# Rebuilding the front of a DFT and MLP kernel: x loads first, one casting queue for the weights, a turn by chunks of lines, and a low-rank step in column tiles

## The chip, the cores and the metric

The kernel runs on one core of one Trainium2 chip. The metric is the device time of one execution in microseconds (us). Most executions of one kernel agree within a few tenths of a per cent; the median is quoted with its range. "Faster" or "slower" means by more than 2%. The "granted clock" is the share of TensorE's full speed that the chip allowed, as the trace records it; the "span" runs from the first to the last instruction of the profiled execution.

## The reference

For eight sequences of 3136 rows and 256 columns the reference takes the real part of a two-dimensional DFT, adds a low-rank mix along the sequence, and then a two-layer MLP with a residual:

```python
def reference(x, U, V, w_ch1, w_ch2):         # x (8, 3136, 256); U (3136, 32); V (32, 3136)
    X = np.fft.fft(np.fft.fft(x, axis=1), axis=2).real
    u = X + ((X.transpose(0, 2, 1) @ U) @ V).transpose(0, 2, 1)
    return u + np.maximum(u @ w_ch1, 0) @ w_ch2       # w_ch1 (256, 1024), w_ch2 (1024, 256)
```

## The kernel before

The 3136-point DFT is split as 49 times 64. Four names recur in the profile:

- `xs -> ps -> z`: stage 1. The first pair of sequences is loaded sequence by sequence, each in four chunks, by loads that cast f32 to bf16. The Trainium skill ("DMA: Bandwidth & Descriptors", section "SWDGE vs HWDGE vs iDMA") says that only DMAs issued from GpSimd can cast. In this trace all casting loads are in one queue, q0; the transfers that SP issues are in q1.
- `z -> zturn -> g`: the turn. z is written to HBM and read back with the other axis on the partitions.
- `teps -> te`: the low-rank step on TensorE, copied ("spread") into the lower half of g. Its weights are made from U: `us` for a single sequence, and `UZ`, the same values sent through HBM (`uturn`), for a pair.
- `g, T -> ps -> q`, then `hps -> hT -> ops -> om -> out`: stage 3 and the MLP.

The front, which is everything before the first MLP matmul (hps), is a hand-made order. Here are the parts that matter, with cuts marked:

```python
    nc.sync.dma_start(out=U_f, in_=moe_U...)            # plain f32, SP's queue
    nc.sync.dma_start(out=uv[64:96], in_=moe_V)
    part[0][1] = load_single(0, 1)                      # x of sequence 0: casting loads from GpSimd
    part[0][2] = load_single(0, 2)
    ...                                                 # chunks 3 and 0; GpSimd: copies of V into T, iotas, mask
    s1b0[2](); s1b0[3]()                                # stage 1; every second step writes z to zturn
    nc.sync.dma_start(out=w1_f[:], in_=moe_w_ch1...)    # W1 behind the first z writes on SP's queue
    ...
    s1b0[6](); s1b0[7]()
    ...
    nc.vector.tensor_tensor(w1s[:, 0], w1_f[:, 0], w1_f[:, 1], op=AL.add)
    nc.vector.tensor_tensor(w1s[:, 1], w1_f[:, 0], w1_f[:, 1], op=AL.subtract)
    turn(first, 0, [(0, 8), (8, 16), (16, NK1)], [nc.sync, nc.scalar])   # read g, after all z writes
    keep_warm(8)
    ...                                                 # W1 fold on TensorE; W1p out
    bp_sin = residual_tables()
    nc.gpsimd.tensor_copy(w2_f[0:64, 0, 0, 0:3], first.g[0][0:64, 7:NK1:8, 0])   # W2 waits for g
    nc.sync.dma_start(out=w2_f, in_=moe_w_ch2...)
    te_single(first, 0, spread_first)                   # low-rank step, then stage 3
    ...
    for c in (1, 2, 3, 0):
        part[1][c] = load_single(1, c)                  # x of sequence 1, behind the copy that waits for g
```

`keep_warm` issues matmuls whose results nobody uses, to keep TensorE busy; `residual_tables` makes the sine table `Bp` of the residual's matmuls (`ops<-Bp,q`). The low-rank step multiplies cosine and sine parts together and masks what is not wanted:

```python
    for j in range(lo, hi):                             # one pair of sequences: 32 matmuls of 256 columns
        nc.tensor.matmul(st.ps[:, 0, :], UZ[:, j], pr.z[:, j], start=(j == 0), stop=(j == 31))
    ...
    nc.vector.tensor_tensor(te[64:128, :], ps[hb, 0, :], mask[hb, :], op=AL.mult)
```

Of the kernel before, what the change touches and what calls it, by code (L numbers as in the profile page):

```python
# [8 lines left out]
BF16 = mybir.dt.bfloat16  # L9
# [13 lines left out]
def kernel(  # L23
# [19 lines left out]
    ud = nc.dram_tensor("uturn", (NK1, 2, 32, 64), BF16, kind="Internal").ap()  # L43
# [14 lines left out]
    Fs = cpool.tile([PR, 9, 32, 2], FP16)  # L58
# [9 lines left out]
    mask = cpool.tile([P, D], FP32)  # L68
# [117 lines left out]
    def s1_single(pr, b, tiles, evacs, engines):  # L186
# [5 lines left out]
        zdb = zd[pr.p % 2, b]  # L192

        def step(n, s):
# [3 lines left out]
            for i in range(2):  # L198
                o = ps[64 * i:64 * i + 64]
                if s == 0 and i == 0:  # L200
                    todo.append([(o[:, 1], xs[:, 1], 0), (o[:, 0], xs[:, 0], 1), (o[:, 0], x32[b][:], 2)])
                else:
                    todo.append([(o, xs[:, l + 2 * i:l + 2 * i + 2], 0)])
            prods = []
            for parts in todo:
                pp = []
                for o, y, t in parts:
                    fe, fo, fn = (Fs[:, 3 * t + i].rearrange("p k c -> p (k c)") for i in range(3))
                    pp += [(o[..., 0:129], fe, y[..., 0:129]), (o[..., 1:128], fe, y[..., 255:128:-1]),
                           (o[..., 129:256], fo, y[..., 1:128]), (o[..., 129:256], fn, y[..., 255:128:-1])]  # L210
                prods.append(pp)
# [6 lines left out]
            if n % 2:  # L218
                q = s // 2
                for i in range(2):  # L220
                    dst = bass.AP(zd.tensor, zdb.offset + (8 * q + 2 * i) * D, [[32 * D, 64], [4 * D, 2], [1, 2 * D]])
                    engines(n)[i].dma_start(out=dst, in_=z[64 * i:64 * i + 64, 4 * q:4 * q + 4].rearrange(
                        "p (i h) d -> p i (h d)", h=2))
# [4 lines left out]
    def turn(pr, b, parts, engines=(nc.sync,)):  # L228
        g = gpool.tile([P, NK1, D], BF16, tag=f"g{b}", name="g")
        src = zd[pr.p % 2, b].rearrange("k cn d -> cn k d")  # L230
        for i, (k0, k1) in enumerate(parts):
            engines[i % len(engines)].dma_start(out=g[0:64, k0:k1], in_=src[:, k0:k1, :])
        pr.g[b] = g

    def te_out(pr, b, ps, hb, spread):
        te = ypool.tile([P, D], BF16, tag="te", name="te")
        nc.vector.tensor_tensor(te[64:128, :], ps[hb, 0, :], mask[hb, :], op=AL.mult)  # L237
        spread(pr.g[b], te)

    def te_steps(pr, spread):  # L240

        st = Obj()

        def step(lo, hi):
            if lo == 0:
                st.ps = psd.tile([P, 2, D], FP32, tag="ps", name="teps")
            for j in range(lo, hi):
                nc.tensor.matmul(st.ps[:, 0, :], UZ[:, j], pr.z[:, j], start=(j == 0), stop=(j == 31))  # L248
            if hi == 32:
                for b in range(2):  # L250
                    te_out(pr, b, st.ps, slice(64 * b, 64 * b + 64), spread)

        for lo, hi in [(0, 11), (11, 22), (22, 32)]:
            yield lambda lo=lo, hi=hi: step(lo, hi)

    def te_single(pr, b, spread):

        ps = psd.tile([P, 2, D], FP32, tag="ps", name="teps")
        for k in range(NK1):
            nc.tensor.matmul(ps[0:64, 0, :], us[:, k], pr.g[b][0:64, k, :], start=(k == 0), stop=(k == NK1 - 1))  # L260
        te_out(pr, b, ps, slice(0, 64), spread)
# [144 lines left out]
    uv = tmp([P, S], "uv")  # L406
    U_f = uv[0:64, 0:N1 * R]
    nc.sync.dma_start(out=U_f, in_=moe_U.rearrange("(k2 k1) r -> k2 (k1 r)", k1=N1))
    nc.sync.dma_start(out=uv[64:96], in_=moe_V)
    first = Pair(0)  # L410
    part = [[None] * 4, [None] * 4]
    part[0][1] = load_single(0, 1)
    part[0][2] = load_single(0, 2)
    an2 = tmp([PR, 2, 3, 32, 2], "an2")
    nc.gpsimd.memset(an2[:], 192.0)
    part[0][3] = load_single(0, 3)
    nc.gpsimd.memset(x32[0][:].bitcast(FP32), 0.0)
    part[0][0] = load_single(0, 0)

    Vk = uv.rearrange("p (k2 k1) -> p k1 k2", k1=N1)  # L420
    for lo, hi in [(0, 9), (9, 17), (17, NK1)]:
        nc.gpsimd.tensor_copy(T[64:96, lo:hi, 0:64], Vk[64:96, lo:hi, :])
    kio = UZ[0:64].rearrange("p a b -> p (a b)").bitcast(I32)[:, 0:64 * NK1].rearrange("p (k j) -> p k j", j=64)

    nc.gpsimd.iota(kio, pattern=[[1, NK1], [N1, 64]], base=0, channel_multiplier=0)
    nc.gpsimd.iota(kio[32:33, 0:NK1:2], pattern=[[0, 13], [1, 64]], base=0, channel_multiplier=0)
    nc.gpsimd.iota(kio[32:33, 1:NK1:2], pattern=[[0, 12], [-1, 64]], base=63, channel_multiplier=0)
    nc.gpsimd.memset(mask[:], 0.0)
    for b in range(2):
        nc.gpsimd.memset(mask[64 * b:64 * b + 32, 0:129], 1.0)  # L430
        nc.gpsimd.memset(mask[64 * b + 32:64 * b + 64, 129:256], 1.0)

# [33 lines left out]
    ans = tmp([PR, 3, 32, 2], "ans")  # L466
    for tab, c, off in [(0, 0, 192.25), (0, 1, 192.5), (1, 0, 1), (1, 1, 2), (2, 0, 3), (2, 1, 4)]:
        ts(ans[:, tab, :, c], jf[0:PR, 0:32], pv[:, 0:1], off if off > 100 else pv[:, off:off + 1])
# [5 lines left out]
    ub = tmp([64, N1, R], "ub", BF16)  # L474
    nc.scalar.copy(ub[:].rearrange("p k r -> p (k r)"), U_f)
# [9 lines left out]
    ts(ta[:, :, 0:32], tb[:], 32.25, None, AL.add)  # L485
    ts(ta[:, :, 32:64], tb[:], 32.0, None, AL.add)
    ts(alt[:, 1:2], ph[:], 0.5, 32.25)
    ts(alt[:, 2:3], ph[:], -0.5, 32.75)
    nc.vector.tensor_copy(ta[:, 0:NK1:2, 32], alt[0:64, 1:2].to_broadcast([64, 13]))
    nc.vector.tensor_copy(ta[:, 1:NK1:2, 32], alt[0:64, 2:3].to_broadcast([64, 12]))  # L490
    mask_bits(ta[:], 18)
    ups = psh.tile([P, 2, 512], FP32, tag="h", name="ups")
    for i in range(2):
        nc.tensor.matmul(ups[0:64, i, 0:384], jm[:], ub[:, NK1 + 12 * i:37 + 12 * i].rearrange("p k r -> p (k r)"),
                         start=True, stop=True)
    keep_warm(4)
    rv = tmp([64, 2, 12, 2, R], "rv", BF16)
    ups_v = ups[0:64, :, 0:384].rearrange("p i (k r) -> p i k r", k=12)
    nc.scalar.copy(rv[:, :, :, 0, :], ups_v)
    ua = tmp([64, NK1, 64], "ua", FP16)  # L500
    nc.scalar.copy(T[64:96, 1:NK1, 64:128], Vk[64:96, 48:24:-1, :])



# [4 lines left out]
    ts(jq[:, 0, 65:P], jf[:, 2:P:2], pl[:], 128.5)  # L509
    ts(jq[:, 1, 0:64], jf[:, 1:P:2], pl[:], 128.25)  # L510
    ts(jq[:, 1, 64:P], jf[:, 1:P:2], pl[:], 128.5)
    mask_bits(jq[:], 16)

    w1_f = tmp([P, 2, H], "w1_f")
    A, V = copy_act, copy_dve
    s1b0 = list(s1_single(first, 0, part[0], [A, V, A, V, A, V, A, A],
                          lambda n: (nc.sync, nc.scalar if n == 7 else nc.sync)))
    s1b0[0]()
    sin_of(ua[:], ta[:], 18)
    s1b0[1]()  # L520
    keep_warm(4)
    ts(rv[:, :, :, 1, :], ups_v, -1.0, None)


    ts(m[:], h, -1.0, 1.0)
    ts(pv[:, 5:6], u[:], m[:], None)
    ts(pv[:, 6:7], u[:], 24.0 / 49, m[:], AL.subtract, AL.mult)
    for i, off in enumerate([0.25, 0.0, 0.5]):
        ts(pv[:, 7 + i:8 + i], m[:], off, 192.0)
    s1b0[2]()  # L530
    s1b0[3]()
    nc.sync.dma_start(out=w1_f[:], in_=moe_w_ch1.rearrange("(h p) j -> p h j", p=P))
    keep_warm(4)
    for i in range(2):
        for t in range(3):
            ts(an2[:, i, t, :, i], jf[0:PR, 0:32], pv[:, 5 + i:6 + i], pv[:, 7 + t:8 + t])
    mask_bits(an2[:], 16)
    Q = tmp([P, 2, P], "Q", FP32R)
    sin_of(Q[:], jq[:], 16)
    sin_of(Fs[:, 3:9], an2[:].rearrange("p a t k c -> p (a t) k c"), 16)  # L540


    pn = tmp([64, 2], "pn")
    ts(pn[:, 1:2], pf[0:64], 32.0, 32.0, AL.is_ge, AL.mult)
    ts(pn[:, 0:1], pf[0:64], pn[:, 1:2], 1.0 / S, AL.subtract, AL.mult)
    ts(pn[:, 1:2], pn[:, 1:2], -0.25 / 32, 32.25)
    nc.vector.memset(pn[32:33, 0:1], 0.5)
    nc.vector.memset(pn[32:33, 1:2], 32.25)
    ta2 = kio.bitcast(FP32)
    s1b0[4]()  # L550
    s1b0[5]()
    ts(ta2, kio, pn[:, 0:1], pn[:, 1:2])
    mask_bits(ta2, 18)

    for k0, k1 in [(0, 16), (16, 25)]:
# [9 lines left out]
        if k0:  # L565
            copy_dve(us[:, k0:k1], ps[0:64, 0:k1 - k0])
        else:
            ups0 = ps
    s1b0[6]()
    s1b0[7]()  # L570
    copy_act(us[:, 0:16], ups0[0:64])
    nc.vector.tensor_copy(T[96:128, :, 0:64], T[64:96, :, 0:64])
    ts(T[96:128, 1:NK1, 64:128], T[64:96, 1:NK1, 64:128], -1.0, None)
    w1s = tmp([P, 2, H], "w1s", FP32R)
    nc.vector.tensor_tensor(w1s[:, 0], w1_f[:, 0], w1_f[:, 1], op=AL.add)
    nc.vector.tensor_tensor(w1s[:, 1], w1_f[:, 0], w1_f[:, 1], op=AL.subtract)
    turn(first, 0, [(0, 8), (8, 16), (16, NK1)], [nc.sync, nc.scalar])
    sin_of(T[0:64, :, 0:64], ta2, 18)
    nc.vector.tensor_copy(T[0:64, :, 64:128], T[0:64, :, 63::-1])
    keep_warm(8)  # L580

    for c in range(2):
        cs = slice(c * 512, (c + 1) * 512)
        ps = psh.tile([P, 2, 512], FP32, tag="h", name="w1ps")
        for blk in range(2):
            nc.tensor.matmul(ps[:, blk], Q[:, blk], w1s[:, blk, cs], start=True, stop=True)
        if c:
            ts(W1p[:, :, cs], ps[:], 0.5, None)
        else:
            nc.scalar.mul(W1p[:, :, cs], ps[:], 0.5)  # L590
    keep_warm(8)
# [165 lines left out]
```

## Time and profile before

| | before |
|---|---|
| time, median of 3 runs | 471.02 us (469.86 to 472.12) |
| profiled run | 474.89 us, span 473.1 us, mean granted clock 0.978 |
| first hps | 38.40 us |

The profiled execution of before lies about 4 us above the median, that of after (below) about 3, so differences between single profiles are good to a few microseconds only.

First, busy time by stretch of the span. The columns are the stretch, its length, the busy time (and instructions) of each engine (TensorE's matmuls, its weight loads, VectorE, ScalarE, GpSimd), the granted TensorE clock, the DMA share and the GB/s. Before:

```profile
0.00:40.00 40.00, 29.82 (x212) 16.26 (x213) 29.91 (x88) 17.79 (x21) 22.18 (x39) 0.82 0.86 176
40.00:60.00 20.00, 18.75 (x174) 12.17 (x173) 9.26 (x18) 13.03 (x18) 6.99 (x14) 0.94 0.76 149
60.00:460.00 400.00, 392.82 (x3256) 283.95 (x3255) 183.53 (x401) 254.78 (x346) 110.04 (x91) 1.00 0.55 142
```

From 60 to 460 us the matmul engine (first busy column) works 393 of 400 us at full clock: it bounds. The first 40 us are different: 30 of 40 us busy, many of those keep-warm matmuls, at a mean clock of 0.82. That is the front, and a microsecond saved there is a microsecond of the whole.

Next, the chain of waits of before (start, length, what), cut to the front:

```profile
2.17 8.81 DMA xs<-in_x_dram
...
17.73 5.76 DMA w_f<-in_moe_w_ch_dram
...
24.73 1.15 DVE w1s L576
...
31.01 3.43 PE teps L260 x25
...
38.40 3.68 PE hps L334 x8
```

Read it as: the first x chunk lands at 11.0 us; W1, issued behind the z writes at 17.7, lands at 23.5; two adds, the fold, warm-up matmuls, the low-rank step; the MLP begins at 38.4. What SP issued in that time (start, length of the group, what, count), before:

```profile
13.21 4.47 SPq L222 DMA_DIRECT2D zturn<-z  x4
17.73 0.60 SPq L532 DMA_DIRECT2D w_f<-in_moe_w_ch_dram  x1
19.50 2.26 SPq L222 DMA_DIRECT2D zturn<-z  x3
24.85 1.27 SPq L232 DMA_DIRECT2D g<-zturn  x2
```

The reads of g are issued at 24.9 us, and TensorE's list of waits has none for g; the longest behind stage 1 is the one for the adds on W1:

```profile
PE w1ps L586 <- DVE w1s L575: 2.5, 1, 2.5
```

By the landing signals (the semaphore updates of each transfer that the trace records) the last piece of g is there at 31.5 us, while TensorE is at the first of its 25 teps matmuls. The eight z writes, of 128 KB each, took 2.7 to 4.5 us from issue to landing.

Last, the steps of the low-rank matmuls of one pair (32 matmuls in three slices), and of the single second sequence, before:

```profile
125.91 1.36 PE L248 MATMUL teps<-z,UZ 128*128 128x256 bf16 x11
...
130.73 1.25 PE L248 MATMUL teps<-z,UZ 128*128 128x256 bf16 x10
```

```profile
74.42 2.91 PE L260 MATMUL teps<-g,us 64*64 64x256 bf16 x25
```

### The profile page before, as it was taken

How to read it: one execution, taken by the hardware profiler on the slowest of the kernel's cores; microseconds unless marked ns; L12 is line 12 of the kernel's file. 1: busy time of each engine (PE TensorE's matmuls, PEld its weight loads, DVE VectorE, ACT ScalarE, POOL GpSimd, SP SyncE). 2: the span in 40 equal slices, each digit the busy share in tenths (PEclk: the TensorE clock that was granted, in tenths of full speed). 3: DMA queues.
4: the chain of work that ended last, by engine and by line, in shares of the span. 5: the costliest groups of instructions: out<-in, count | busy, mean ns of one | idle time of the engine just before them, and what ended most of it. 6: DMA issues, size and time to landing. Idle time of an engine off the chain costs nothing.

```text
span 473.1 us, 9455 instructions
## 1 busy us (share of the span) xinstructions
PE 446.1 (94%) x3685; PEld 316.4 (67%) x3685; DVE 225.0 (48%) x512; ACT 287.5 (61%) x387; POOL 139.2 (29%) x143
## 2 busy tenths in 40 slices
PE   5878988999999999999999989999999999999992
PEld 2544666767867767677867767667867777767672
DVE  8856343785326366544145376555245345122111
ACT  6526564767655657777465657777465655666660
POOL 8433506872160155352060245452130000000000
PEclk9877999999999999999999999999999999999998
DMA  9969577777594367584592357574762222232323
GB/s 157 216 142 168 147 163 195 205 220 210 157 190 127 101 168 208 160 240 123 142 219 70 102 159 209 156 240 130 167 135 62 69 63 65 65 78 73 79 62 74
DMA packets 69297, 67.63 MB, mean 143 GB/s; under 512 B 17396, under 2 KB 62268, under 8 KB 69220
## 3 DMA queue, kind: packets, MB, share of 16 engines
q1 hardware_dynamic: 55252, 47.43, 40.8%
q0 software_dynamic: 11168, 12.92, 12.2%
q10 hardware_dynamic: 2832, 6.69, 4.0%
q8 instruction: 29, 0.48, 0.4%
q14 instruction: 16, 0.13, 0.1%
HBM read 35.95 MB, written 34.28 MB: 148 GB/s over the span
## 4 chain that ended last, share of the span: by engine, by line
PE 73%; DMA 9%; DVE 7%; ACT 4%; issue 2%; SPq 2%; POOL 1%; DVEq 0%; POOLq 0%; ACTq 0%
PE hps L334 29%; PE ops L345 29%; PE ps L283 4%; PE ops L348 4%; DMA xa<-in_x_dram 3%; PE teps L248 2%; ACT hT L336 2%; PE ps L172 2%; DMA xs<-in_x_dram 2%; DMA out_dram<-ob 2%; SPq L360 2%; DVE q L79 1%; DMA xb<-in_x_dram,idx 1%; DMA w_f<-in_moe_w_ch_dram 1%; PE ps L216 1%
## 5 line engine op out<-in xcount | busy, mean ns | idle before, releaser
L336 ACT ACTIVATE hT<-hps 128x1024 bf16<-128x1024 f32 (+1 forms) x208 | 202.5, 975 | 134.4 <-PE hps L334 132.3
L345 PE MATMUL ops<-W,hT 128*128 128x256 bf16 x1568 | 224.4, 273 | 0.3 <-DVE W L628 0.3
L345 PEld LDWEIGHTS <-hT 128*128 128x128 bf16 x1568 | 145.1, 98 | 34.2
L355 DVE TENSOR_TENSOR ob<-ops,om 128x256 f32<-128x256 f32 (+1 forms) x100 | 41.8, 418 | 182.3 <-ACT om L354 177.3
L334 PE MATMUL hps<-q,W1p 128*128 128x512 bf16 (+1 forms) x448 | 106.6, 360 | 1.7 <-DVE q L79 1.4
L334 PE MATMUL hps<-q,W1m 128*128 128x512 bf16 x384 | 98.0, 379 | 0.5 <-ACT hT L336 0.5
L131 POOL TENSOR_TENSOR y<-xa,xb 98x1020 f32<-98x1020 f32 (+1 forms) x24 | 54.7, 2278 | 126.0 <-DMA xa<-in_x_dram 119.9
L79 DVE CAST q<-ps 128x512 bf16<-128x512 f32 (+3 forms) x120 | 64.4, 558 | 31.0 <-PE ps L283 27.4
L334 PEld LDWEIGHTS <-W1p 128*128 128x128 bf16 x448 | 41.1, 98 | 28.6 <-issue 4.5
L334 PEld LDWEIGHTS <-W1m 128*128 128x128 bf16 x384 | 35.7, 98 | 26.5 <-issue 1.6
L348 PEld LDWEIGHTS <-q 128*128 128x128 bf16 x392 | 38.3, 98 | 21.3 <-issue 0.6
L76 ACT CAST z<-ps 128x512 bf16<-128x512 f32 x57 | 33.5, 587 | 15.8 <-PE ps L172 10.4
L354 ACT COPY om<-ops 128x256 f32<-128x256 f32 (+1 forms) x100 | 36.8, 368 | 8.5 <-PE ops L345 8.2
L283 PE MATMUL ps<-T,g 128*128 128x128 bf16 (+1 forms) x400 | 38.3, 223 | 3.5 <-DVE g L267 1.3
L356 DVE TENSOR_TENSOR ob<-ops,om 128x256 f32<-128x256 f32 (+1 forms) x100 | 40.8, 408 | 0.0
L348 PE MATMUL ops<-Bp,q 128*128 128x128 f16 x200 | 38.4, 219 | 0.0
L267 POOL COPY g<-te 64x1024 int32<-64x1024 int32 (+1 forms) x21 | 21.7, 1076 | 51.9 <-DVE te L237 30.8
L348 PE MATMUL ops<-Bm,q 128*128 128x128 f16 x192 | 36.9, 219 | 0.0
L283 PEld LDWEIGHTS <-g 128*128 128x128 bf16 x400 | 30.3, 100 | 8.9 <-DVE g L267 1.6
L122 DVE TENSOR_TENSOR yb<-y 98x508 bf16<-98x508 f32 (+1 forms) x24 | 31.6, 1317 | 3.0 <-POOL y L131 2.9
L102 POOL DMA_INDIRECT xb<-in_x_dram,idx x24 | 25.5, 1063 | 5.3 <-issue 4.4
L172 PE MATMUL ps<-yb,F 98*128 98x258 bf16 (+1 forms) x108 | 18.9, 265 | 3.6 <-DVE q L79 3.4
(127 smaller groups left out, 216.3 us busy)
## 6 DMA issues: line engine op xcount, KB each, us to landing
out_dram<-ob SPq DMA_DIRECT2D x392, 64.0 KB
xa<-in_x_dram SPq DMA_DIRECT2D x24, 392.0 KB
g<-zturn SPq DMA_DIRECT2D x7, 800.0 KB
zturn<-z ACTq DMA_DIRECT2D x9, 512.0 KB
xs<-in_x_dram POOLq DMA_DIRECT2D x16, 196.0 KB, 8.7
w_f<-in_moe_w_ch_dram SPq DMA_DIRECT2D x2, 1024.0 KB
zturn<-z SPq DMA_DIRECT2D x15, 128.0 KB
zturn<-z ACTq DMA_DIRECT2D x3, 448.0 KB
```

Of the source, the lines that this page charges most:

```text
L76: nc.scalar.copy(o, i)
L79: nc.vector.tensor_copy(o, i)
L122: nc.vector.tensor_tensor(o[:, :, 1:128], i[:, :, 1:128], i[:, :, 255:128:-1], op=AL.add)
L131: nc.gpsimd.tensor_tensor(ck.y[:, 0:n, 1:256], ck.xa[:, 0:n, 1:256], rb[:, :, 255:0:-1], op=AL.add)
L283: nc.tensor.matmul(o, lt, r, start=st, stop=True, skip_group_check=True)
L334: nc.tensor.matmul(ps[:, i, 0:n], (W1p if ch.sg > 0 else W1m)[:, blk, j], q[:, blk, c0:c0 + n], start=(blk == 0), stop=(blk == 1))
L336: nc.scalar.activation(ch.h[:, 2 * jp:2 * jp + 2, 0:n], ps[:, :, 0:n], AF.Relu)
L345: nc.tensor.matmul(ps, ch.h[:, j, t * P:(t + 1) * P], W2[:, j, :], start=(j == 0 and t % 2 == 0), stop=(j == JT - 1), skip_group_check=True)
L348: nc.tensor.matmul(ps[:, j], q[:, j, tk], (Bp if ch.sg > 0 else Bm)[:, j], start=False, stop=False, skip_group_check=True)
L354: nc.scalar.copy(om[:, 0:n], ch.po[:, 0:n, 1])
L355: nc.vector.tensor_tensor(ob[:, 0:n, 0:P], ch.po[:, 0:n, 0], om[:, 0:n], op=AL.add)
L356: nc.vector.tensor_tensor(ob[:, 0:n, P:D], ch.po[:, 0:n, 0], om[:, 0:n], op=AL.subtract)
```

## The change

The intent: x is the head of the chain, so it should load first. U, V, W1 and W2 follow it in the one casting queue, where casting also saves copies and allows W1 to be folded straight on TensorE without the two adds. The turn goes in four groups of lines, each read as soon as it is written, in long contiguous runs. And the low-rank step computes only the two column ranges it needs, as two column tiles side by side. The diff also moves sequence 0's turn, in part on ScalarE's queue before, to SP's alone, reads the later pairs' turns in two pieces per sequence, reorders the columns of some tables, and cuts a pair's low-rank step into two slices. The core of the diff (shortened):

```diff
-    nc.sync.dma_start(out=U_f, in_=moe_U...)
-    nc.sync.dma_start(out=uv[64:96], in_=moe_V)
     ...                                        # x of sequence 0, four chunks
+    nc.gpsimd.dma_start(out=ub[:]..., in_=moe_U...)          # casting to bf16
+    nc.gpsimd.dma_start(out=vb[64:96], in_=moe_V)
+    for c in range(2):
+        nc.gpsimd.dma_start(out=w1_f[:, :, cs], in_=w1_v[:, :, cs])     # float32r
+    nc.gpsimd.dma_start(out=w2_f, in_=moe_w_ch2...)
     ...                                        # GpSimd's copies of V into T
+    for c in (1, 2, 3, 0):
+        part[1][c] = load_single(1, c)         # x of sequence 1: here, no longer after g
     s1b0[2](); s1b0[3]()
+    turn_single(first, 0, 8, 16)               # read these lines as soon as they are written
     s1b0[4](); s1b0[5]()
+    turn_single(first, 0, 16, 24)
     s1b0[6](); s1b0[7]()
+    turn_single(first, 0, 24, 32)
+    turn_single(first, 0, 0, 8)
     ...
-    nc.vector.tensor_tensor(w1s[:, 0], ...)  # and the subtraction: W1 now in 8 matmuls instead of 4
-    bp_sin = residual_tables()                 # was before te_single
     te_single(first, 0, spread_first)
     ...
-    bp_sin()
+    residual_tables()()                        # now after the first stage-3 steps
@@ low-rank step
-    nc.tensor.matmul(st.ps[:, 0, :], UZ[:, j], pr.z[:, j], ...)
+    for s, cs in enumerate([slice(0, 129), slice(129, 256)]):
+        nc.tensor.matmul(st.ps[64 * s:64 * s + 64, 0, cs], UZ[:, j, s::2], pr.z[:, j, cs], ...)
@@ load_uz: what two DMAs of 50 partitions did
+    for c in range(2):                         # per sequence: four of 25 partitions
+        nc.sync.dma_start(out=UZ[64 * b + c:64 * b + 2 * NK1:2, :, ...], in_=ud[:, :, 1 - c, :])
```

## The prediction

> **What bounds the kernel now.** The engine summary has the matmul engine busy 94%. The table by stretch of time separates two regimes. From 60 to 460 us it is busy 394 of 400 us at full clock: it bounds. Before that is a front: by the timeline the first MLP matmul (hps) starts at 38.4 us, and the granted clock falls to 0.5 in 12-14, 26-32 and 36-42 us. The chain of waits there reads: first x chunk lands at 10.98 us; W1 is issued behind the z writes at 17.7 and lands at 23.5; two VectorE adds (2.4 us); W1 fold, warm-up matmuls; low-rank step (teps) 31.0-34.4; spread, s3; hps. The turned g of sequence 0 is issued at 24.9, after the last z write, and its first user starts at 31.6. DMA engines are about 0.9 busy through the front.
>
> **What changes.**
> 1. U and V (0.8 MB) no longer go ahead of x. At about 300 GB/s of source bytes (estimate from the x and W1 landings) x lands 2.5-3.5 us earlier: first chunk near 7 us, last near 14.
> 2. The turn is cut into four groups of lines, read in 12.8 KB runs while x still arrives; z is written in 512 B runs instead of 1 KB. g should be complete near 22-23 us instead of about 31.
> 3. W1 goes behind x, U, V in the casting queue. Everything ahead of or beside it (x 3.2 MB read, U/V 0.8, z 1.0, g 0.6, W1 1.0) at about 0.3 MB/us puts it at 24-26 us: no earlier than now. That becomes the new last wait of the front. The adds go, four float32r matmuls come (0.2 us each warm, 0.45 cold).
> 4. teps in the front: 25 matmuls of 256 columns (3.4 us, half cold) become 50 of about 128 columns in two column tiles, estimate 1.5 us warm. From W1's landing to hps I count 1.3 fold + 1.3 warm-up + 1.5-2.5 teps + 4 te, spread, s3, q = about 8.5 us: hps at about 33.5 us, 5 us earlier (3 to 7).
> 5. In the bound regime, every saved matmul microsecond counts. teps there is 96 matmuls at 107 ns spacing plus 25 more: 13 us. Two column tiles run together in this trace already: s1 of the single sequences takes 0.63 us for 8 matmuls of 256 columns, drain included, half of serial. The Trainium skill ("TensorE: Matmul & The Clock Gate", Part 3) says the same of column tiles. But weight loads double, and this trace's 64-column matmul/load pairs (uups) come no closer than 33 ns, so I expect about 2 us per pair instead of 3.5, less mode switches: 4 to 5 us in all.
> 6. W2 and the second sequence's x arrive earlier; that removes only 0.3 us of matmul wait on the W2 fold. UZ's loads split into four of 25 partitions; I expect no critical wait.
>
> **Sum.** 5 + 4.5 + small = about 11 us.
>
> Predicted time **460 us**, 8 in 10 within **454 to 466**. Chances: faster by over 2% 0.60, within 2% 0.38, slower 0.02.
>
> **What would show it.** First hps at 31-36 us; the chain before it through the W1 load, not through x or g; g complete before W1; teps on UZ at 1.7-2.3 us per pair (now 3.5); matmul busy time between hps and the end about 5 us less; the end moved by the sum.
>
> **What would make it wrong.** Column tiles not overlapping when each matmul has its own load (lose 4.5 us). W1 landing at 28 us or later, from sharing engines with the 512 B z writes, so the front gains nothing. A longer cold-clock stretch while PE waits for W1. Or W1 much earlier (22 us), giving 456.

## The result, and the profile after

| | before | after |
|---|---|---|
| time, median | 470.80 us (469.86 to 472.12, 4 runs) | 487.46 us (485.82 to 490.76, 4 runs) |
| ratio, 95% interval | | 1.0361 (1.0301 to 1.0421): slower |
| profiled run | 474.89 us, clock 0.978 | 490.76 us, clock 0.954 |
| first hps | 38.40 us | 52.40 us |
| first output (om) | 52.0 us | 69.0 us |

The median of before is over one run more than in the table above. A ratio is the mean time of one kernel's fast runs over that of the other's fast runs of the same rounds, so it is not quite the ratio of the medians.

The same stretches, after:

```profile
0.00:40.00 40.00, 23.88 (x162) 13.53 (x165) 24.26 (x69) 15.04 (x15) 26.67 (x41) 0.76 1.06 180
40.00:60.00 20.00, 9.70 (x85) 6.32 (x87) 7.21 (x21) 4.14 (x7) 0.00 (x0) 0.59 0.22 25
```

From 40 to 60 us TensorE is busy 9.7 us instead of 18.8, at a mean clock of 0.59. The chain of waits, after:

```profile
16.32 10.77 DMA zturn<-z
...
27.52 9.47 DMA zturn<-z
37.01 8.30 DMA g<-zturn
45.45 2.89 PE teps L271 x47
...
58.58 1.87 PE hps L346 x4
```

W1 is not in it; it had landed at 25.6 us. One z write takes 10.8 us, the next 9.5, the last read of g 8.3. TensorE's longest waits, after (who waited for what: total, times, longest):

```profile
PE teps L271 <- DMA g<-zturn: 12.9, 1, 12.9
...
PE hps L346 <- ACT hT L348: 2.5, 1, 2.5
```

What SP issued from 20 us on, after:

```profile
20.86 0.34 SPq L238 DMA_DIRECT2D g<-zturn  x1
21.30 0.37 SPq L222 DMA_DIRECT2D zturn<-z  x1
27.11 0.32 SPq L238 DMA_DIRECT2D g<-zturn  x1
27.52 0.38 SPq L222 DMA_DIRECT2D zturn<-z  x1
32.52 4.81 SPq L238 DMA_DIRECT2D g<-zturn  x2
```

SP issues in order. A read waits for the landing of its write, and the next write stands behind that read: the fourth write was ready at 21.3 us and was issued at 27.5. What filled the DMA engines meanwhile is in the queue shares for 27 to 37 us, after (packets, MB, share of 16 engines; shares of overlapping packets can pass 100% together):

```profile
q0 software_dynamic: 2543, 1.08, 91.4%
q1 hardware_dynamic: 649, 0.69, 33.8%
```

The casting queue q0, with the second sequence's x, holds 91% while the turn's last write and reads are in q1.

The low-rank step, after: the first 20 of a pair's 32 column pairs, and the single second sequence:

```profile
145.82 1.32 PE L257 MATMUL teps<-z,UZ 128*64 128x129 bf16 x40
```

```profile
91.48 1.88 PE L271 MATMUL teps<-g,us 64*32 64x129 bf16 x50
```

With 0.87 us for the other 12 a pair takes 2.19 us instead of 3.97: shorter, as predicted. And SP's issue of the UZ loads, of before and then of after:

```profile
103.64 3.83 SPq L666 DMA_DIRECT2D UZ<-uturn  x2
```

```profile
121.04 9.72 SPq L661 DMA_DIRECT2D UZ<-uturn  x4
```

To see where the difference arises I compared the times of the hundred output copies (om) of both traces, k-th with k-th. After minus before: +14.0 us at the first hps, +17.1 at the first om, +18.5 at the seventh, +19.8 at the sixteenth, then 1.2 to 1.4 less at each of the three later pairs, +16.1 at the end. So the front loses 14, the stretch right behind it 6, and the low-rank step gives back almost 4.

### The profile page after: what moved, and what is told of

Read it like the earlier page. It is cut to its first block, busy times and chain, and to the rows that moved or that the text cites. A ratio compares the mean times of both kernels' runs of the same rounds, so it can differ in the third digit from the quotient of the medians.

```text
span 489.0 us, 9686 instructions
## 1 busy us (share of the span) xinstructions
PE 440.6 (90%) x3767; PEld 313.9 (64%) x3829; DVE 220.2 (45%) x520; ACT 286.3 (59%) x385; POOL 140.8 (29%) x143
## 4 chain that ended last, share of the span: by engine, by line
PE 72%; DMA 10%; DVE 8%; ACT 4%; issue 3%; SPq 1%; POOL 1%; DVEq 0%; POOLq 0%; ACTq 0%
PE ops L357 30%; PE hps L346 30%; DMA zturn<-z 4%; PE ps L295 4%; PE ops L360 4%; DMA xa<-in_x_dram 3%; PE ps L173 2%; ACT hT L348 2%; DMA g<-zturn 2%; DVE q L80 2%; SPq L372 1%; DMA xb<-in_x_dram,idx 1%; PE teps L257 1%; PE ps L217 1%; DVE ob L367 1%
## 5 line engine op out<-in xcount | busy, mean ns | idle before, releaser
L346 PE MATMUL hps<-q,W1p 128*128 128x512 bf16 (+1 forms) x420 | 105.3, 361 | 6.0 <-ACT hT L348 2.5
L346 PE MATMUL hps<-q,W1m 128*128 128x512 bf16 x353 | 96.3, 382 | 2.0 <-ACT hT L348 0.5
L123 DVE TENSOR_TENSOR yb<-y 98x508 bf16<-98x508 f32 (+1 forms) x24 | 23.6, 983 | 5.6 <-POOL y L132 5.5
L103 POOL DMA_INDIRECT xb<-in_x_dram,idx x24 | 24.5, 1020 | 5.3 <-issue 4.4
```

The lines of the kernel that those rows point to most:

```text
L346: nc.tensor.matmul(ps[:, i, 0:n], (W1p if ch.sg > 0 else W1m)[:, blk, j], q[:, blk, c0:c0 + n], start=(blk == 0), stop=(blk == 1))
```

## The experiments

The theory after reading the traces: the early loads of sequence 1's x (and W2, W1), which before waited for g, now share the DMA engines with the turn and stretch it; SP's order makes it worse; residual tables and UZ loads add a little. Rivals: the new turn format itself (512-byte pieces, gathers of lines) is slow; or W1, now cast, is late.

All kernels gave correct results. "First hps" is read from each profile.

| run | what it is | median us | ratio (95% interval) | first hps |
|---|---|---|---|---|
| after | | 487.46 | 1.0361 (1.0301 to 1.0421) | 52.40 |
| e1_x1_late | after, x of sequence 1 waits for g | 480.16 | 1.0183 (1.0118 to 1.0247) | 43.17 |
| e2_turn_last | after, the reads behind all writes | 483.13 | 1.0238 (1.0166 to 1.0310) | 47.21 |
| e5_tables | after, residual tables early again | 483.90 | 1.0260 (1.0181 to 1.0338) | 49.12 |
| e3_both | e1 and e2 | 477.21 | 1.0093 (1.0030 to 1.0157) | 41.09 |
| e6_all3 | e1, e2 and e5 | 475.10 | 1.0035 (0.9977 to 1.0094) | 41.62 |
| e7_w2_late | e6, W2 after g | 471.52 | 0.9960 (0.9902 to 1.0017) | 37.34 |
| e8_before_x1_early | before, x of sequence 1 early | 484.41 | 1.0217 (1.0158 to 1.0277) | 47.89 |
| e9_uz_two | e7, UZ in pieces of 50 partitions | 470.58 | 0.9946 (0.9907 to 0.9986) | 38.90 |
| e10_one_read | e9, g in one read | 468.89 | 0.9931 (0.9897 to 0.9965) | 38.41 |
| e11_w1_late | e10, W1 behind GpSimd's copies of V | 473.81 | 1.0022 (0.9983 to 1.0061) | 42.93 |
| e13_w1_sp | e10, W1 as in before | 472.74 | 1.0000 (0.9963 to 1.0037) | 40.43 |
| e14_iota_late | e13, GpSimd's iotas later | 471.65 | 0.9986 (0.9957 to 1.0015) | 41.83 |
| e4_te_only | before with the column-tiled step | 467.75 | 0.9914 (0.9852 to 0.9976) | (slow) |
| e12_te_again | the same again | 468.95 | 0.9931 (0.9883 to 0.9979) | 34.64 |
| e15_x_first_only | e12, U and V behind x | 482.53 | 1.0215 (1.0165 to 1.0265) | 50.52 |

### e1_x1_late: the second sequence's x after g again

```diff
-    for c in (1, 2, 3, 0):
-        part[1][c] = load_single(1, c)        # right behind the copies of V
     ...
+    nc.gpsimd.tensor_copy(gw[:], first.g[0][0:64, 7:NK1:8, 0])      # GpSimd waits for g, as before
+    for c in (1, 2, 3, 0):
+        part[1][c] = load_single(1, c)
     te_single(first, 0, spread_first)
```

> The changed kernel with one thing undone: the second sequence's x loads leave the casting queue until the first turn (g) has landed. Contention theory (the casting queue's backlog makes each z write and g read take 8 to 11 us): g complete at 33 to 36 us instead of 45.4, first hps near 41 to 43 instead of 52.4, time about 476 to 479 (10 us under the changed kernel). Issue-order theory (SP waits for one z write to land before it issues the next): the last z write is still issued near 27 us, so at most 4 us gained, about 484. Format theory (512 B writes and 16-partition reads are slow by themselves): no gain, 487.

Measured: 480.16 us, 1.0183; first hps 9.2 us earlier than in after. The chain of waits of e1_x1_late:

```profile
16.65 11.68 DMA zturn<-z
28.76 3.81 DMA zturn<-z
32.59 3.51 DMA g<-zturn
```

The last write falls from 9.5 to 3.8 us and the last read from 8.3 to 3.5 once nothing else is in the casting queue. The one at 16.65, still beside U, V, W1 and W2, takes 11.7 us (10.8 in after). By the medians this move is worth 7.3 us, the largest single part of the loss.

### e2_turn_last: the four reads behind the four writes

```diff
     s1b0[3]()
-    turn_single(first, 0, 8, 16)
     ...                                    # and the second
-    turn_single(first, 0, 24, 32)
-    turn_single(first, 0, 0, 8)
+    for n0 in (8, 16, 24, 0):
+        turn_single(first, 0, n0, n0 + 8)
```

> The changed kernel with the four reads of the turn issued after all four z writes. Issue-order theory: the last z write is issued near 21.5 us instead of 27.5 and everything after moves up by 6 us: about 481. Contention theory: the writes are issued earlier but still take 9 to 11 us each among the casting queue's packets, and the reads meet the second sequence's x: gain 0 to 4 us, 483 to 487. Format theory: no gain.

Measured: 483.13 us, 1.0238. The chain of waits of e2_turn_last:

```profile
19.66 10.66 DMA zturn<-z
30.34 9.80 DMA g<-zturn
```

The writes are no longer held behind reads: the fourth goes out at 19.7 instead of 27.5. It then takes 10.7 us, and the reads 9.8, because the casting queue is full. Issuing reads early, meant to overlap the turn with x, cost 4 to 5 us (medians, first hps) in the shared order of SP.

### e4_te_only and e12_te_again: the column-tiled step alone

Here the kernel before gets only the diff's low-rank step (the matmuls in two column tiles, te copied in two pieces without the mask, us in the order that this needs).

> The kernel before with the column-tiled low-rank step alone. My accounting of the traces (teps 2.15 us per pair instead of 3.5, single 1.8 instead of 2.8, both in stretches where the matmul engine bounds; front teps 1.5 to 2 us shorter): 5 to 7 us faster than before, 464 to 466. Rival (mode switches, doubled weight loads and two VectorE copies give it back, as the changed kernel's sum suggests: it gained only 1 us from first hps to the end): within 1.5 us of before.

> The kernel before with the column-tiled step alone, once more beside the rebuilt fronts and for a profile in the fast state: 4 us under before, ratio 0.990 to 0.993; the profile shows teps at 2.2 us per pair and first hps within 1 us of 38.4.

Measured: 467.75 us (0.9914) and, on another chip, 468.95 us (0.9931). The profile of the second is read. One pair in e12_te_again:

```profile
123.44 0.81 PE L250 MATMUL teps<-z,UZ 128*64 128x129 bf16 x22
...
127.55 0.76 PE L250 MATMUL teps<-z,UZ 128*64 128x129 bf16 x20
```

A pair costs 2.38 us instead of 3.97, the single sequence 1.59 instead of 2.91. The outputs end 5.3 us earlier in the profiled run; 3 to 4 us by the medians, less than the 5 to 7 expected of e4. Of the 3.8 us at the first hps, the shorter teps in the front explains 1.3. This part of the change is a gain on its own. Twice as many matmuls, each of half the columns, take 0.6 of the time, so the tiles overlap.

### e5_tables: the residual tables before the low-rank step again

```diff
+    bp_sin = residual_tables()
     te_single(first, 0, spread_first)
     ...
-    residual_tables()()
+    bp_sin()
```

> The changed kernel with the residual tables computed before the low-rank step again, as the kernel before has it. If the 2.5 us wait of hps on hT at 56 us comes from these tables on VectorE and their sine ahead of hT on ScalarE: that wait goes and the cold clock after it too, 2.5 to 4 us faster than the changed kernel, about 484. If the wait only hides another: under 1 us.

Measured: 483.90 us, 1.0260. From first hps to the first om 13.5 us instead of 16.6. In after, the tables' twelve VectorE operations and their sine stood between stage 3 and the first hT (TensorE's 2.5 us wait for hT in the list above). The diff moved them into the only stretch where they are on the chain. My prediction did not mention this move.

### e3_both and e6_all3: together

> The changed kernel with both: second sequence's x after g, and the reads of the turn after all four z writes. If backlog and issue order are two separate losses: the last z write goes out at about 20 us instead of 28.8, and g is complete near 31 us instead of 36: 475 to 477, 4 us under the run with x late alone (480.2). If the backlog of W1 and W2 alone holds the writes (each still 9 to 12 us, the last landing near 31): g near 34, 478.

> The same plus the residual tables ahead of the low-rank step. If the table wait is additive it takes off another 3 us: about 473. If, with g earlier, the tables still collide with W1's scaling on VectorE: 1 us or less.

Measured: 477.21 us (1.0093) and 475.10 us (1.0035). e1 and e2 nearly add up: 10 us together by the medians (7.3 and 4.3 alone), where the casting queue now carries only U, V, W1 and W2 beside the turn. The tables are worth another 2 us. The last write still takes 8.7 and 7.2 us in these two profiles.

### e7_w2_late: W2 too

```diff
-    nc.gpsimd.dma_start(out=w2_f, in_=moe_w_ch2...)
     ...
+    nc.gpsimd.tensor_copy(w2_f[0:64, 0, 0, 0:3], first.g[0][0:64, 7:NK1:8, 0])
+    nc.sync.dma_start(out=w2_f, in_=moe_w_ch2...)                  # as before
```

> The same plus W2 taken out of the casting queue and loaded on SP after g, so that only x, U, V and W1 are ahead of the turn. Contention theory: the last two z writes (9 to 12 us before) shrink to 3 to 6 us, g complete near 28 to 30 us, first hps at 36 or earlier, and with the column-tiled step's 4 us the kernel beats the one before: 464 to 468. Rival (W1, not W2, is what the writes wait behind, or W2 now late for the fold): 470 to 474.

Measured: 471.52 us, 0.9960, first hps at 37.3 us. With W2's 1 MB out of the way the last write takes 6.0 us. As a time this is a miss: it lies in the range given for the rival, and W1 is still beside the turn.

### e8_before_x1_early: the reverse test

The kernel before, with all its formats, but the four loads of sequence 1's x moved ahead of the wait for g.

> The reverse test: the kernel before, with only the second sequence's x loads issued early, right after the first's and ahead of the turn. Contention theory: z writes and the g read of the first sequence, with their old formats and old order, now stretch to 8 us and more, W1 lands late too, first hps moves from 38 to 45 or later: 477 to 483. If the new formats or the new order are what hurts: the kernel stays within 2 us of before, 469 to 473.

Measured: 484.41 us, 1.0217. The low-rank step waits 7.7 us for g. The chain of waits, e8_before_x1_early:

```profile
20.21 7.59 DMA zturn<-z
27.86 10.48 DMA g<-zturn
```

This single move makes the kernel before lose about 11 us by the medians of its rounds. In before there was no wait of TensorE for g, and the reads were done in 6.6 us (24.85 to 31.48). So the rival, that the new format of the turn is slow, is not needed. It is also contradicted by the trace of after itself: the second sequence uses the same format later, when the DMA engines are idle. For 62 to 69 us, after, the GB/s in 40 equal slices:

```profile
GB/s 0 0 0 0 0 0 0 0 0 0 0 0 0 0 0 0 0 0 0 0 0 0 181 298 287 293 287 152 0 0 0 0 0 0 0 0 0 0 94 290
```

The 256 KB of one z write move there at almost 300 GB/s in about one microsecond (2.3 us from issue to the last landing signal).

### e9_uz_two and e10_one_read: the UZ loads, and one read of g

e9 lays out the HBM copy of u so that UZ is loaded by two DMAs of 50 partitions, as before (storing u then takes two DMAs); e10 also replaces the four reads of g by one of 64 partitions.

> The run with x late, reads last, tables early and W2 late, plus the UZ loads as two of 50 partitions again instead of four of 25. In the traces the four hold SP for 9.3 to 9.7 us (the two: 3.8 to 5.2), the next x load goes out late, and the kernel loses about 2 us between its 12th and 15th pair of output copies. If that is the cause: the loss goes, first hps unchanged, ratio to before 0.990 to 0.993 (it was 0.996). If the loss belongs to the shifted schedule: no change.

> The same with the turn of the first sequence read by one DMA of 64 lines instead of four of 16. The last of the four took 5.4 us for 205 KB with nearly nothing else on the engines. If reads of 16 partitions are slow because few engines or ports take part: one read of 64 lines lands within 4 to 5 us of the last write, first hps 0.5 to 1.5 us earlier. If the early groups' overlap is worth more: up to 1 us later.

Measured: 470.58 us (0.9946) and 468.89 us (0.9931). SP's issue of the UZ loads, e7_w2_late and then e9_uz_two:

```profile
101.14 9.30 SPq L661 DMA_DIRECT2D UZ<-uturn  x4
```

```profile
103.08 6.02 SPq L661 DMA_DIRECT2D UZ<-uturn  x2
```

SP is held 6.0 instead of 9.3 us. Between the thirteenth and the sixteenth output, e7 lost 2.4 us against before (from -2.35 to +0.05), and e9 nothing (-0.27 to -0.26): the x load behind UZ came 13.4 us after the one ahead of it in e7 and 11.4 us in e9. The other traces agree: all seven kernels with four pieces lose 1.7 to 4.2 us there, and none with two pieces more than 0.6, though the time that two pieces hold SP varies from 3.8 us (before) to 7.8 us (e12). The Trainium skill ("DMA: Bandwidth & Descriptors", section "Why a DMA increments its semaphore by 16 and not by 1") says that the number of engines of a transfer is the largest one up to 16 that divides the slowest dimension of both sides: 5 for 25 partitions and 10 for 50. The trace agrees: after one signal 0.4 us behind the issue, each of e7's loads is followed by 5 landing signals, and each of e9's by 10 (the z writes, on 128 partitions, have 16). Why fewer engines should hold SP longer is not shown. The intervals of e7, e9 and e10 overlap; only the profiles tell them apart. One read instead of four is within the noise. Nor did its long runs speed it up: e10's read of g took 6.4 us, the three of before 6.6.

### e11_w1_late: W1 behind the copies of V

> The same with W1 issued some 7 us later in the casting queue, after the V copies, so that the last z writes meet only x, U and V. Contention theory: the last two z writes take 3 to 4 us instead of 6 to 9, g lands 2 us earlier, W1 lands near 27 and folds while g is read; first hps 1 to 3 us earlier, ratio 0.984 to 0.990. Rival (W1 becomes the last wait): first hps no earlier or later than without.

Measured: 473.81 us, 1.0022: worse. The read of g was issued at 23.6 us, 2.7 us earlier than in e10, so W1's transfer does stretch the turn: the last z write, in the same 512-byte pieces, took 2.4 us (21.2 to 23.5) instead of e10's 6.1. But then W1 itself is last (TensorE waits 4.0 us for it). Against e10, of the same rounds, the order costs 4.9 us, and the intervals do not overlap.

### e13_w1_sp: W1 off the casting queue

W1 goes back to SP's queue in plain f32, behind the first z writes, with the two adds and four matmuls of before.

> The repaired rebuild (one 64-line turn read, two UZ pieces, W2 and the second sequence's x after g) with W1 moved back off the casting queue: plain f32 on the hardware queue behind the z writes, the two VectorE adds and the plain 4-matmul fold of the kernel before. Theory (a transfer on the casting queue beside the turn is what stretches it): the last z write takes about 3.5 us, as in the kernel before with the column-tiled step, instead of 6.1 us; the 64-line read is issued near 23.5 us and lands near 29; first hps near 35-36 us; ratio near 0.987. Rival (loading x first gives nothing even without the queue's contention, because the V copies and the casts then end later): first hps near 38 us, ratio 0.993 or worse.

Measured: 472.74 us, 1.0000. A miss. The chain of waits of e13_w1_sp:

```profile
7.56 10.24 DMA xs<-in_x_dram
...
24.57 3.47 ACT T L568
28.07 0.55 DVE T L393
28.65 1.23 DVE w1s L574
```

The adds on W1 no longer wait for W1. They stand on VectorE behind the copies of T, which wait for ScalarE's copy of V. That starts at 24.6 us, behind work on U; U and V, now behind x, landed at 18.9 and 20.0 us (5.1 and 7.3 in before). In before, the copy was done at 10.9, while x was still loading. And the last z write, now with no cast beside it after 20 us, was no faster than e10's 6.1 us (7.7 us; in e14, with the same loads, 5.9 us, 20.1 to 26.0). The GB/s from 18 to 27 us in e14_iota_late, in 40 slices:

```profile
GB/s 365 329 379 253 272 241 209 300 389 371 385 380 396 344 353 355 401 314 239 250 228 107 118 96 73 39 59 32 25 23 20 20 23 23 2 0 0 0 0 0
```

It runs out in a tail of some 20 GB/s, which is what 512-byte packets of 27 ns, one after another, give: in the packet records, one DMA engine finishing alone. e12 has no such tail (its last z packets are done by about 23.3 us). The landing signals narrow it down. Of the 16 signals of e13's U, 15 came by 17.0 us and the last at 18.9; of W1's, 15 by 23.9 and the last at 26.2; of the last z write's, 15 by 25.5 and the last at 27.6. So in each of them one share in 16 is late, from U on (in before, U's 16 signals came within 0.6 us). In e10, e13 and e14 the last z write ended 1.4 to 1.6 us after W1, whichever queue W1 was in; in e11, with W1 issued behind it, it took 2.4 us. Which engine is late, and why, these records do not tell; that stays open.

### e14_iota_late: VectorE and GpSimd

In after, two VectorE copies of 64 by 13 and 64 by 12 values took 1.7 and 1.6 us, while GpSimd ran an iota. After:

```profile
9.99 1.70 DVE L514 COPY ta<-alt 64x13 f32<-64x13 f32 x1
...
11.74 2.42 DVE L384 TENSOR_SCALAR ta<-ta 64x1600 int32<-64x1600 int32 x1
```

e14 is e13 with the iotas moved behind GpSimd's copies of V, and what reads them moved down.

> The same with GpSimd's iotas moved behind the V copies. Theory (VectorE's small strided copies of 1.6 us and its mask of 2.4 us are held up while GpSimd runs the iota): the copies fall back to about 0.17 us and the mask to about 1.0 us, z of the first chunk is ready 1.5 to 3 us earlier, first hps up to 2 us earlier than in the run beside it. Rival: T's sine, whose input now comes later, becomes the new last wait of the front, and the run is 0 to 2 us slower than the run beside it.

Measured: 471.65 us, 0.9986, not separable from e13. The same instructions in e14_iota_late:

```profile
9.97 0.20 DVE L507 COPY ta<-alt 64x13 f32<-64x13 f32 x1
...
10.73 0.97 DVE L384 TENSOR_SCALAR ta<-ta 64x1600 int32<-64x1600 int32 x1
```

The mechanism is as expected. The Trainium skill ("SBUF — State Buffer", section "Who interferes with whom") says that VectorE and GpSimd can block each other for a whole instruction on a shared pair of ports, when VectorE works in a mode that uses both. The trace does not show the mode, but its times agree: 1.7 us with the iota beside it, 0.2 without. But z of the first chunk was not what the last z write waited for, which was issued at 20.1 us all the same. The saved time was off the chain.

### e15_x_first_only: the order of loads alone

The rebuilt front with every repair (e10, 0.9931) was no better than the kernel before with the column-tiled step (e12, 0.9931). In both, the last z write is issued at 20.1 us. So is loading x first worth anything? e15 is e12 with one edit:

```diff
-    nc.sync.dma_start(out=U_f, in_=moe_U...)
-    nc.sync.dma_start(out=uv[64:96], in_=moe_V)
     ...                                       # the loads of x
+    nc.gpsimd.dma_start(out=U_f, in_=moe_U...)
+    nc.gpsimd.dma_start(out=uv[64:96], in_=moe_V)
```

> The kernel before with the column-tiled step, and of the rebuild only this: U and V, still plain f32, are issued by GpSimd behind the first sequence's x instead of ahead of it on the hardware queue. Theory (U and V ahead of x cost x almost nothing: they were through by about 5.4 us, at more than 200 KB a microsecond, while the casting queue alone gives x about 150 KB a microsecond): the first x chunk lands near 8 us instead of 9.8 to 11, but the last x chunk lands no more than 1.5 us earlier than without the edit, V lands 6 us or more later, the last z write is issued within 1 us of 20.1 us, and the ratio is 0.993 or worse. Rival (the prediction: U and V ahead of x held all of x back by 2.5 to 3.5 us): the last z write is issued near 17.5 us and the ratio is near 0.987.

Measured: 482.53 us, 1.0215. The expectation for the z write was a miss, and as a test of the time the run is spoiled: TensorE's order has the matmul on U ahead of most of stage 1, so everything waited for U until 20.3 us, and the last z write came at 33.8. That only says that U must not be late in this order of work.

But the question about x can be read from its packets. I counted the 1813 data packets of sequence 0's x (512 or 4096 bytes, 1.63 MB written as bf16) in the trace of each kernel, with the time at which a share of the bytes was done:

| kernel | first packet | half done | 90% done | last |
|---|---|---|---|---|
| before | 5.2 us | 10.5 | 14.9 | 16.7 |
| e12_te_again | 5.3 | 10.4 | 14.9 | 16.2 |
| after | 2.8 | 9.5 | 13.9 | 17.0 |
| e10_one_read | 2.9 | 9.7 | 14.1 | 17.3 |
| e15_x_first_only | 2.9 | 9.8 | 14.1 | 17.5 |

With U and V out of the way, x starts 2.4 us earlier, is 0.7 to 1.0 us ahead at half and 0.8 to 1.1 at 90%, and ends 0.3 to 1.2 us later. The share of the queues from 2 to 6 us shows the start, before and then after:

```profile
q1 hardware_dynamic: 128, 0.80, 83.6%
q0 software_dynamic: 151, 0.10, 16.7%
```

```profile
q0 software_dynamic: 919, 0.32, 68.9%
```

Before moved 0.80 MB of U and V and the beginning of x in these 4 us. After moved 0.32 MB of x: x starts slowly (71, 137 and 92 KB in the microseconds from 3, 4 and 5, against 130 to 160 from 6 us on). At the end, U and V, queued behind x, run alongside it, from 12 us on, with a quarter of x still to come: from 14 to 17 us the x packets of after fill 10.5, 4.0 and 0.7 engines on average while other packets of q0 fill 6.5, 9.0 and 10.9. In e15 no z write was in flight then, and x's tail was as long. So putting U and V behind x did not bring x's end forward; that much the packets show. That what runs beside x's tail takes back the lead it still has at 90% is argued: a front with nothing beside that tail was not run, and no run shows the time of an otherwise equal kernel.

## Why the prediction was wrong

It said 460 us with 0.02 for slower; the result was 487.5, slower by 3.6%.

1. *Step 1, "x lands 2.5-3.5 us earlier: first chunk near 7 us, last near 14".* Right for the first chunk (used at 7.8 us instead of 11.0), wrong for the last (last packet at 17.0 us instead of 16.7). The bytes of U and V were divided by a rate, and x's slow start and the crowded end were not in the sum. g needs the last chunk, and the intended gain does not appear: the last z write is issued at 20.1 us in e10, with x first, and in e12, without.
2. *Step 2, "g should be complete near 22-23 us".* This is the step that failed worst: g was complete at 45.3 us. It needed z writes as quick as those of before (2.7 to 4.5 us) beside a casting queue that by then held U, V, W1, W2 and a second x. They took 9 to 11 us, and the reads 7 to 9 (e1, e2 and the reverse test e8 show it), and SP's order put the last write behind a read (e2). The Trainium skill ("DMA: Bandwidth & Descriptors", section "Queues, rings and completion order") says that each DMA engine takes turns between the queues it has work for, packet by packet. A turn of 1 MB with a backlog beside it then gets a share of each engine and no priority, and the queue shares above agree in direction: q0 91%, q1 34%.
3. *Step 3, "that [W1] becomes the new last wait".* The time of W1 was right (24 to 26 us predicted, 25.6 measured), the wait was not: in after, TensorE waits 12.9 us for g and has no wait for W1 in its list. W1 as last wait came true only in e11, when W1 was issued late.
4. *Step 4, the way from W1 to hps, 8.5 us, and hps at 33.5.* The way starts from g instead: hps at 52.4. The clock, at 0.50 from 36 to 54 us after TensorE had stood idle from 32.5 us, lengthened it: teps took 2.9 us instead of the 1.5 to 2.5 in the sum, and the same 50 matmuls take 1.9 at full clock later. The move of the residual tables was overlooked; e5 shows about 3 us.
5. *Step 5, column tiles worth 4 to 5 us.* Right in mechanism, a little high in size: e4 and e12 gain 0.7 to 0.9%, 3 to 4 us by medians, and 5.3 in the profile. The Trainium skill ("TensorE: Matmul & The Clock Gate", Part 3) says that column tiles run together, and 3.97 us against 2.38 for the same work agrees.
6. *Step 6, W2 and the second x "arrive earlier", UZ with "no critical wait".* The first half named the cause of the loss and counted it as harmless: they arrive earlier by taking engine time from the turn. The second half was wrong by about 2 us (the profiles of e7 and e9).

The prediction did name "sharing engines" among what would make it wrong, but for W1 as the victim and for no more than the loss of the gain. What it missed is that before held these loads back on purpose: the little GpSimd copy out of g ahead of W2 and of the second x was the guard that kept the engines free for the turn.

What stays open: why the last z write of the repaired fronts takes about 6 us (e10, e13, e14) where e12's takes 3.5; e11 ties it to W1, but why one share in 16 is late is seen, not explained. The front also varies by 2 to 3 us from run to run (e12's first hps is 3.8 us before that of before, and 1.3 of it is teps), so differences of that size between single profiles are not relied on. No version is over 2% faster than before; e12 (before with the column-tiled step alone) and e10 both reach 0.993, and e12 is the simpler one.

## What to carry to other kernels

Before moving a load earlier, ask which transfers run at that time and whether one of them is on the chain: an early load that nobody waits for takes engine time from one that somebody does, and an odd wait ahead of it may be what protects that one. To judge "this first", look at when the *last* piece lands, not the first, and at what the queue's rate is in its first microseconds. Where one engine issues both writes and the reads that depend on them, put all writes first.

## What the Trainium skill lacked or had wrong

- "DMA: Bandwidth & Descriptors" gives no rate for a casting transfer. Here x, in packets of 512 and 4096 bytes, moved at 110 to 200 KB of bf16 written per microsecond, and in after, e10 and e15, where it comes first, at 65 to 141 in its first three full ones. W1 moved up to 395 KB in a microsecond in the casting queue (e11) as well as plain on SP's (before), so being in the casting queue does not by itself set the rate.
- The same page says that an engine takes turns between queues, but not what that costs a short transfer beside a long backlog: from issue to landing a 256 KB write took 9 to 12 us with the casting queue full (after, e1, e2), 3.8 (e1) and 2.4 us (e11) with it empty, and 2.3 us with all engines idle.
- The same page lists no time for which a DMA holds its issuing engine by shape: SP was held 9.3 to 9.7 us for four loads on 25 partitions (e7, after) and 3.8 to 7.8 us for two on 50 with the same bytes (before, e9, e10, e12).
- "TensorE: Matmul & The Clock Gate" has figures for three column tiles of 512 columns, none for short ones with a weight load each: two tiles of about 128 columns ran 1.67 times as fast as one matmul of 256 (3.97 and 2.38 us per pair).
